# In-place bias rows for the first head, and other moves at the start of an attention and SwiGLU kernel

## The chip, the cores and the metric

The kernel runs on one core of a Trainium2 chip. The metric is the device time of one execution in microseconds (us), as the median over several runs. The profile was taken from one of these executions.

## The reference, cut to what matters

The inputs are q, k, v of shape (8, 8, 576, 64) and s of shape (8, 8, 576): 8 batches of 8 heads, 576 positions, 64 columns per head. The three weight matrices are 512x1536, 512x1536 and 1536x512.

```python
scores = scale * np.matmul(q, k.transpose(0, 1, 3, 2))
s_pos = np.maximum(s, 0.0)
cum = np.cumsum(s_pos, axis=-1)
bias = -(cum[:, :, :, None] - cum[:, :, None, :])
scores = np.where(causal, -1000000000.0, scores + np.minimum(bias, 0.0))
attn = np.exp(scores - np.max(scores, axis=-1, keepdims=True))
attn = attn / (np.sum(attn, axis=-1, keepdims=True) + 1e-09)
x = np.matmul(attn, v)        # heads side by side: 4608 tokens x 512
out = (silu(x @ w_gate) * (x @ w_val)) @ w_out
```

So each score gets a bias that is the difference of two running sums of s, one of the key's position and one of the query's.

## The kernel before

**Tiles.** 64 pairs of batch and head are counted from 0 to 63 (`bh`); head n below means such a pair. Four heads make a half batch (`HB = 4`): heads 0 to 3 are half batch 0, heads 4 to 7 half batch 1, and so on. Queries and keys of a half batch lie transposed in two tiles `KQ[hb % 2][r]`, r = 0 or 1 (lines 91 to 94; in the program kq00 and kq10 for even half batches, kq01 and kq11 for odd ones). Each has 128 partitions, a query part (index 0) and a key part (index 1) of 2 x 576 + 64 columns. The two heads of a row r lie side by side: head e = 0 in columns 0 to 575, head e = 1 in columns 576 to 1151. In tile r the 64 data rows are partitions 64r to 64r + 63. The other 64 are bias rows: four of them hold numbers, the others hold zeros.

**Bias.** The running sums, times 8, are kept in `HL` (64 partitions, one per head) as two bf16 numbers, a high part and the rest, beside rows of 1 and -1. Lines 226 to 232 compute it on VectorE: clamp and scale (226), running sum (227), high part (230), rest (231), and a copy of both for the query side (232). `aug(hb, engs)` (lines 178 to 186) sends to each head four bias rows from `HL` by a DMA (line 183): with the ones and minus ones beside the sums, the score matmul itself adds key sum minus query sum. All four rows of one head are one DMA of 9 KB.

**Scores.** `score_piece(bh, ci)` (lines 338 to 381) computes a head's scores in four pieces, keys on the partitions. `CHUNKS` (lines 56 to 61) lists per piece the blocks of 128 keys and the range of queries. A piece takes a PSUM bank, lays the causal mask into it with a matmul of `lower` (line 353, pieces 0 and 3 of the first 8 heads), adds the scores (line 359), and ScalarE turns it into exps (line 369), which gives the bank back. The fourth piece (`ci = 3`) holds key block 4, and its key operand is always 128 columns wide:

```python
T[:, 1, e * S + 128 * tj : e * S + 128 * (tj + 1)]
```

**Ways into the tiles.** q and k are loaded with positions on partitions and turned by TensorE: for half batch 0 in halves, `row_half(nm, r, eng)` (lines 886 to 890), by transposes into PSUM (line 301) and copies out to `KQ` (lines 314 and 316) on the named engine; for half batch 1 by `half_batch(nm)` (lines 892 to 895, line 287), the r = 0 copies at once, the r = 1 copies by the loop at lines 940 to 942. Half batches 2 to 4 use `prep_one` (line 527), half batch 3 at the places in `PREP_AT` (lines 536 to 539), keyed by half batch and then by the head and piece after which a part stands. Later ones are turned by DMA. `pe_out` copies for both rows share a bank: it is given back after the r = 1 copy. V is loaded in five pieces of 128 positions (`load_v`, line 157) and cast to bf16 with a column of ones beside it (`cast_v`, line 168; `init_vt` sets ones and zeros, lines 189 to 191).

**Order.** The schedule is written out by hand: every engine runs its instructions in the order in which the program lists them, and waits are put in for the data. The first 36 us are lines 188 to 232 and 906 to 980: clear and load, warming matmuls on TensorE (`keep_warm`, line 884), half batch 0, then scores of heads 0 to 7 mixed with half batch 1, values (`values`, lines 901 to 904, matmuls at line 396), transposes of the outputs (`x_pe`, line 446) and the first gate products (`begin`, line 630). From line 1004 on a loop over 9 tiles of 512 tokens runs the feed-forward products (lines 630, 687 and 736) and, between them, the attention of heads 8 to 63 by a running balance (`pump`). `at_item` hooks single steps to items of the first tile: the casts of half batch 3 are hooked to items 7 and 8. PSUM has eight banks; `take()` gives the bank that was given back longest ago.

SyncE issues the DMAs of `nc.sync`: s (line 188), k and q of half batch 0 in halves (line 140), then the bias rows. GpSimd issues k and q of half batch 1 (lines 221 and 222), V of batch 0 (line 915) and the weights (line 332).

## Time and profile before

| What | Value |
|---|---|
| median of 8 runs | 376.38 us (375.62 to 377.71) |
| the profiled execution | 375.62 us, its span 373.9 us |
| TensorE busy | 361.8 us, 97% of the span |
| VectorE, ScalarE, GpSimd busy | 289.1, 240.8, 212.3 us |
| granted clock of TensorE | 0.999 |

| stretch (us) | TensorE busy | VectorE | ScalarE | GpSimd |
|---|---|---|---|---|
| 0 to 12 | 8.17 | 9.95 | 8.61 | 10.86 |
| 12 to 20 | 6.91 | 6.57 | 7.75 | 7.43 |
| 20 to 28.5 | 8.34 | 5.58 | 6.44 | 7.16 |
| 28.5 to 36.7 | 7.38 | 6.68 | 6.48 | 1.94 |
| 36.7 to 60 | 23.14 | 17.93 | 17.65 | 14.15 |
| 60 to 76 | 15.84 | 7.72 | 11.30 | 11.62 |
| 76 to 118 | 41.45 | 32.49 | 34.10 | 21.15 |

Times inside an execution count from the start of its span. A row of the timeline gives start and length in us, then engine, line, operation, tiles and shapes, and in brackets the idle time just before it and what ended it. PE is TensorE, PEld its weight loads, DVE is VectorE, ACT is ScalarE, POOL is GpSimd, SP is SyncE. A row of the waits gives who waited, after the arrow for whom, then us in total, times and the longest. The chain of work that ended last is followed back from the last instruction, at each step to what released it. Releasers are inferred, and the ends of matmuls are modelled.

### The profile page before, as it was taken

To read this page: it belongs to the slowest core of one execution; us is meant where nothing else is said; L and a number is where in the kernel's file an instruction comes from. 1 tells how busy PE (TensorE), PEld (TensorE's weight loads), DVE (VectorE), ACT (ScalarE), POOL (GpSimd) and SP (SyncE) were. 2 spreads that over 40 slices of the span, in tenths; PEclk is the share of its full clock that TensorE was granted. 3 is DMA by queue.
4 is the path that set the end of the run, shared out by engine and by line. 5 is a ranking of instruction groups with operands and counts; after the bars stand their busy time and mean duration, and the time that the engine had idled before them with its cause. 6 is when DMAs were issued, how large, how long until landed. Compare 5 with 4: busy or idle time off the path is not lost.

```text
span 373.9 us, 8757 instructions
## 1 busy us (share of the span) xinstructions
PE 361.8 (97%) x3259; PEld 230.7 (62%) x3300; DVE 289.1 (77%) x578; ACT 240.8 (64%) x471; POOL 212.3 (57%) x325
## 2 busy tenths in 40 slices
PE   7799999999999999999999999999999999999995
PEld 6575556555555556855685558655865585476464
DVE  7967776368984899589967997699858867975984
ACT  8787876788886877588757875686566523323321
POOL 8982565856355647494649464955675516315320
PEclk9999999999999999999999999999999999999999
DMA  7899999999599997896779675994132103002003
GB/s 239 199 262 262 214 266 267 235 338 199 177 178 278 261 264 196 168 283 217 208 166 266 179 177 167 237 224 110 40 119 62 35 20 127 2 0 96 19 0 114
DMA packets 97146, 64.23 MB, mean 172 GB/s; under 512 B 77232, under 2 KB 82736, under 8 KB 97104
## 3 DMA queue, kind: packets, MB, share of 16 engines
q1 hardware_dynamic: 84976, 41.46, 46.7%
q0 software_dynamic: 12128, 22.21, 22.6%
q8 instruction: 26, 0.43, 0.5%
q14 instruction: 16, 0.13, 0.1%
HBM read 37.90 MB, written 19.86 MB: 154 GB/s over the span
## 4 chain that ended last, share of the span: by engine, by line
PE 92%; POOL 2%; DVE 2%; ACT 1%; issue 1%; DMA 1%; DVEq 0%; POOLq 0%
PE bank L630 48%; PE bank L736 17%; PE bank L359 11%; PE bank L396 8%; PE bank L687 5%; ACT pt L369 1%; DMA kq<-HL 1%; PE bank L287 1%; PE bank L446 1%; DVE kq L316 1%; PE bank L353 1%; DVE pp L653 1%; DVE ht L664 0%; POOL kq L214 0%; POOL rawk L140 0%
## 5 line engine op out<-in xcount | busy, mean ns | idle before, releaser
L369 ACT ACTIVATE pt<-bank 128x512 bf16<-128x512 f32 (+1 forms) x256 | 120.4, 509 | 30.2 <-PE bank L359 17.3
L630 PE MATMUL bank<-XT,wg 128*128 128x512 bf16 x418 | 110.5, 379 | 1.2 <-DVE pp L653 0.3
L630 PE MATMUL bank<-XT,wv 128*128 128x512 bf16 x412 | 109.4, 379 | 1.1
L651 ACT ACTIVATE th<-bank 128x512 bf16<-128x512 f32 x108 | 64.7, 599 | 55.5 <-PE bank L630 50.9
L653 DVE SCALAR_TENSOR_TENSOR pp<-th,bank 128x512 bf16<-128x512 bf16 x108 | 73.7, 682 | 18.9 <-ACT th L651 18.4
L664 DVE SCALAR_TENSOR_TENSOR ht<-pp,bank 128x512 bf16<-128x512 bf16 x108 | 74.2, 687 | 10.3
L359 PE MATMUL bank<-kq 128*128 128x128 bf16 (+4 forms) x576 | 75.9, 240 | 1.8 <-DMA kq<-HL 1.3
L673 POOL TENSOR_TENSOR ht<-ht 128x512 bf16<-128x512 bf16 x35 | 40.4, 1154 | 52.3 <-DVE su L671 52.2
L359 PEld LDWEIGHTS <-kq 128*128 128x128 bf16 x576 | 45.8, 98 | 32.0 <-issue 1.9
L630 PEld LDWEIGHTS <-wv 128*128 128x128 bf16 x432 | 38.3, 98 | 36.1 <-issue 0.2
L630 PEld LDWEIGHTS <-wg 128*128 128x128 bf16 x432 | 38.2, 98 | 34.1 <-issue 0.5
L374 POOL TENSOR_SCALAR_AFFINE_SELECT pt<-pt 128x512 bf16<-128x512 bf16 x56 | 36.8, 658 | 29.3 <-ACT pt L369 23.2
L396 PEld LDWEIGHTS <-pt 128*128 128x128 bf16 x960 | 41.6, 98 | 17.4 <-issue 0.3
L396 PE MATMUL bank<-vt,pt 128*128 128x65 bf16 x960 | 46.7, 194 | 0.1
L430 POOL DMA_DIRECT2D xs<-ot x24 | 21.7, 904 | 30.1 <-DVE ot L413 27.8
L736 PEld LDWEIGHTS <-ht 128*128 128x128 bf16 x336 | 31.1, 98 | 4.3
L413 DVE TENSOR_TENSOR ot<-bank,rc 128x320 bf16<-128x320 f32 x64 | 31.5, 492 | 2.2
L183 POOL DMA_DIRECT2D kq<-HL x48 | 28.9, 605 | 0.0
L736 PEld LDWEIGHTS <-su 128*128 128x128 bf16 x252 | 23.5, 98 | 3.3
L687 PE MATMUL bank<-wo,ht 128*128 128x512 bf16 x90 | 24.8, 380 | 0.3
L412 DVE RECIPROCAL rc<-bank 128x5 f32<-128x5 f32 x64 | 12.1, 189 | 15.4 <-PE bank L396 15.0
L801 POOL TENSOR_TENSOR ysb<-ysb 128x512 f32<-128x512 f32 x12 | 15.2, 1270 | 15.3 <-DVE ysb L795 15.3
(93 smaller groups left out, 387.6 us busy)
## 6 DMA issues: line engine op xcount, KB each, us to landing
out_dram<-ysb POOLq DMA_DIRECT2D x32, 256.0 KB, 4.4
rawv<-in_v_dram SPq DMA_DIRECT2D x28, 256.0 KB
rawk<-in_k_dram SPq DMA_DIRECT2D x12, 576.0 KB
rawq<-in_q_dram SPq DMA_DIRECT2D x12, 576.0 KB
xs<-ot POOLq DMA_DIRECT2D x24, 160.0 KB, 3.6
ks<-ck SPq DMA_DIRECT2D x11, 288.0 KB
qs<-cq SPq DMA_DIRECT2D x11, 288.0 KB
rawk<-in_k_dram POOLq DMA_DIRECT2D x3, 576.0 KB, 6.8
```

The source lines that it names most:

```text
L359: nc.tensor.matmul(sc[:, o : o + w], T[:, 1, e * S + 128 * tj : e * S + 128 * (tj + 1)], T[:, 0, e * S + lo : e * S + hi], start=not maske ...
L369: nc.scalar.activation(pt[:, c0 : c0 + n], sc, AF.Exp, scale=0.125)
L374: nc.gpsimd.affine_select(pt[:, 1088:1600], pt[:, 1088:1600], pattern=[[0, 4], [1, 128]], compare_op=ALU.is_ge, fill=zreg, base=0, channel ...
L396: nc.tensor.matmul(av[:, bi * (D + 1) : (bi + 1) * (D + 1)], pt[:, c0 : c0 + 128], VT[b % 2][:, tj, h, :], start=(tj == 0), stop=(tj == bi),)
L413: nc.vector.tensor_mul(ot[:, :, e * D : (e + 1) * D], av3[:, :, 0:D], rc[:, :, None].to_broadcast([128, NCH, D]),)
L630: nc.tensor.matmul(view(bs, TT), w[:, c, f0 : f0 + 128], xt[:, c, :], start=(c == 0), stop=(c == 3),)
L651: nc.scalar.activation(th, pg, AF.Tanh, scale=0.5)
L653: nc.vector.scalar_tensor_tensor(pp, in0=th, scalar=1.0, in1=pg, op0=ALU.add, op1=ALU.mult)
L664: nc.vector.scalar_tensor_tensor(hp[:, 2 * k2 : 2 * k2 + 2, :].rearrange("p a n -> p (a n)"), in0=pp, scalar=0.5, in1=pv, op0=ALU.mult, op ...
L673: (nc.vector if ft == NFT - 1 else nc.gpsimd).tensor_sub(hp[:, 1:3, :], hp[:, 1:4:2, :], hp[:, 0:3:2, :])
L687: nc.tensor.matmul(view(pys[ts_], DM), hps[ft // 2][:, 2 * (ft % 2) + half, c0 : c0 + 128], WO[j][:, ft % WKO, :], start=(ft == 0), stop=( ...
L736: nc.tensor.matmul(ps, lhs(p), rhs(p), start=(first and p == 0), stop=(last and p == NP - 1), skip_group_check=True,)
```

## The change

`HL`, `s_sb` and `c8` get 98 instead of 64 partitions (`LR = 98`). A second load brings s of head 0 to partitions 64 to 97. A column `less` holds -1, and 0 on partitions 64 and 96, so that the instruction that formed the rest now leaves the high part on partitions 64 and 96 and the rest on 65 and 97. GpSimd copies two rows of these, on the partitions where they lie, into kq00, into the key part (64, 65) and the query part (96, 97); ones and minus ones beside them are set by memsets. `aug(0)` leaves head 0 out. After head 3's scores the rows 96 and 97 of the query part are zeroed again, since later heads use four rows from 64 on.

Beside this: pads of half batch 1 and the ones and zeros of V's tile 0 are set by VectorE instead of GpSimd; the first V piece is issued before the in-place copies and the other four right after the cast of the r = 1 queries, ahead of the memset of kq11's bias rows; one of two r = 1 key copies of half batch 0 goes from ScalarE to VectorE; 16 warming matmuls are dropped; the scores of head 0 stand ahead of the r = 1 query transposes; half batch 1 is turned between the scores of heads 1 to 3 in other places; the values of heads 0 and 1 come after the scores of head 6; half batch 3 is prepared half a head later, its casts one item later.

```diff
@@ -78,6 +78,7 @@
     )
 
     NPE = 5
+    LR = 98
     XB = 2
     KS = {i: dram.tile([NR * S, 128], BF16, name=f"ks{i}") for i in range(NPE, NHB)}
     XS = {
@@ -95,15 +96,16 @@
     VT = [const.tile([128, NCH, H, D + 1], BF16, name=f"vt{i}") for i in range(2)]
     ident = const.tile([128, 128], BF16)
     one_s = const.tile([128, 1], FP32)
-    HL = const.tile([BH, 4, 2, S], BF16)
+    HL = const.tile([LR, 4, 2, S], BF16)
     XR = 3 * TT
     XT = const.tile([128, 4, XR], BF16)
     warm = const.tile([128, 1], FP32)
     WS = const.tile([128, NFT // 2, 3, DM // 2], BF16)
     first_sbuf = ExitStack()
     first = first_sbuf.enter_context(tc.tile_pool(name="first", bufs=1))
-    s_sb = first.tile([BH, S], FP32)
-    c8 = first.tile([BH, S], FP32)
+    s_sb = first.tile([LR, S], FP32)
+    c8 = first.tile([LR, S], FP32)
+    less = first.tile([LR, 1], FP32)
     PTP = {0: first, "bufs": 7}
     lower = first.tile([128, 512], BF16)
 
@@ -180,15 +182,19 @@
                 r, e = divmod(hh, 2)
                 r0 = 64 * (1 - r)
                 bh = hb * HB + hh
+                if bh == 0:
+                    continue
                 engs[hh].dma_start(
                     KQ[hb % 2][r][r0 : r0 + 4, :, e * S : (e + 1) * S],
                     HL[bh : bh + 1, :, :, :],
                 )
 
-        nc.sync.dma_start(s_sb, s.rearrange("b h n -> (b h) n"))
-        def init_vt(i):
-            nc.gpsimd.memset(VT[i][:, :, :, D : D + 1], 1.0)
-            nc.gpsimd.memset(VT[i][64:128, 4, :, 0:D], 0.0)
+        nc.sync.dma_start(s_sb[0:BH, :], s.rearrange("b h n -> (b h) n"))
+        nc.sync.dma_start(s_sb[BH:LR, :], s[0, 0:1, :].to_broadcast([LR - BH, S]))
+
+        def init_vt(i, eng=nc.gpsimd):
+            eng.memset(VT[i][:, :, :, D : D + 1], 1.0)
+            eng.memset(VT[i][64:128, 4, :, 0:D], 0.0)
 
         for r in range(NR):
             load_one(0, "k", (r, r + 1))
@@ -197,8 +203,11 @@
         nc.vector.memset(warm, 0.0)
         nc.vector.memset(one_s, 1.0)
         nc.scalar.activation(warm, warm, AF.Exp)
-        nc.vector.memset(HL[:, 0:2, 0, :].bitcast(FP32), ONES2)
-        nc.vector.memset(HL[:, 2:4, 1, :].bitcast(FP32), NEGS2)
+        nc.vector.memset(HL[0:BH, 0:2, 0, :].bitcast(FP32), ONES2)
+        nc.vector.memset(HL[0:BH, 2:4, 1, :].bitcast(FP32), NEGS2)
+        nc.vector.memset(less, -1.0)
+        for p in (64, 96):
+            nc.vector.memset(less[p : p + 1, :], 0.0)
         make_identity(nc, ident)
         nc.gpsimd.memset(lower, 0.0)
         nc.gpsimd.affine_select(
@@ -206,9 +215,9 @@
             compare_op=ALU.is_ge, fill=nc.gpsimd.to_reg(MASKED), base=0, channel_multiplier=-1,
         )
 
-        def pads(i):
+        def pads(i, eng=nc.gpsimd):
             for r in range(2):
-                nc.gpsimd.memset(KQ[i][r][64 * r : 64 * r + 64, :, NR * S :], 0.0)
+                eng.memset(KQ[i][r][64 * r : 64 * r + 64, :, NR * S :], 0.0)
 
         for r in range(2):
             nc.gpsimd.memset(aug_rows(0, r)[:, 1, :], 0.0)
@@ -216,20 +225,29 @@
                 KQ[0][r][64 * (1 - r) : 64 * (1 - r) + 64, 0, :],
                 one_s[0:64, 0:1].to_broadcast([64, NR * S + 64]), 0.0,
             )
+            if r == 0:
+                nc.gpsimd.memset(KQ[0][0][96:98, 1, 0:S].bitcast(FP32), NEGS2)
         pads(0)
+        nc.gpsimd.memset(KQ[0][0][64:66, 0, 0:S].bitcast(FP32), ONES2)
         nc.vector.memset(aug_rows(1, 0), 0.0)
         for nm in ("k", "q"):
             load_one(1, nm, eng=nc.gpsimd)
-        init_vt(0)
-        pads(1)
+        pads(1, nc.vector)
+        init_vt(0, nc.vector)
+        load_v(0, (0,), nc.gpsimd)
 
         nc.vector.tensor_scalar(s_sb, s_sb, 0.0, 8.0, ALU.max, ALU.mult)
         nc.vector.tensor_tensor_scan(
-            c8, one_s[0:BH, 0:1].to_broadcast([BH, S]), s_sb, 0.0, ALU.mult, ALU.add
+            c8, one_s[0:LR, 0:1].to_broadcast([LR, S]), s_sb, 0.0, ALU.mult, ALU.add
         )
         nc.vector.tensor_copy(HL[:, 0, 1, :], c8)
-        nc.vector.tensor_sub(HL[:, 1, 1, :], c8, HL[:, 0, 1, :])
-        nc.vector.tensor_copy(HL[:, 2:4, 0, :], HL[:, 0:2, 1, :])
+        nc.vector.scalar_tensor_tensor(
+            HL[:, 1, 1, :], in0=HL[:, 0, 1, :], scalar=less, in1=c8,
+            op0=ALU.mult, op1=ALU.add,
+        )
+        for p, kq in ((64, 1), (96, 0)):
+            nc.gpsimd.tensor_copy(KQ[0][0][p : p + 2, kq, 0:S], HL[p : p + 2, 1, 1, :])
+        nc.vector.tensor_copy(HL[0:BH, 2:4, 0, :], HL[0:BH, 0:2, 1, :])
 
         SP4 = [nc.sync] * 4
         GP4 = [nc.gpsimd] * 4
@@ -534,7 +552,7 @@
             seconds.append(lambda: pe_out(hb, nm, g, 1, eng))
 
         PREP_AT = {
-            2: {(1, 0): 0, (1, 2): 2, (2, 0): 1, (2, 2): 3},
+            2: {(1, 2): 0, (2, 0): 2, (2, 2): 1, (3, 0): 3},
             3: {(1, 3): 0, (2, 1): 1, (2, 3): 2, (3, 1): 3},
         }
 
@@ -883,11 +901,11 @@
             for _ in range(n):
                 nc.tensor.matmul(view(spare, 128), ident, ident, start=True, stop=True)
 
-        def row_half(nm, r, eng):
+        def row_half(nm, r, eng, eng1=None):
             for g in range(2):
                 pe_transpose_half(0, nm, g, r)
             for g in range(2):
-                pe_out(0, nm, g, r, eng)
+                pe_out(0, nm, g, r, (eng, eng1 or eng)[g])
 
         def half_batch(nm):
             for g in range(2):
@@ -911,14 +929,14 @@
         row_half("q", 0, nc.vector)
         cast_half(0, "k", 1, nc.scalar)
         cast_half(0, "q", 1, nc.gpsimd)
+        load_v(0, range(1, 5), nc.gpsimd)
         nc.gpsimd.memset(aug_rows(1, 1), 0.0)
-        load_v(0, range(5), nc.gpsimd)
         w_load("g", 0)
         aug(1, SP4)
-        keep_warm(10)
-        row_half("k", 1, nc.scalar)
+        keep_warm(4)
+        row_half("k", 1, nc.scalar, nc.vector)
+        scores(0)
         row_half("q", 1, nc.vector)
-        keep_warm(10)
         cast_one(1, "k", nc.vector)
         cast_one(1, "q", nc.vector)
         for c in range(3):
@@ -931,16 +949,19 @@
         for nm in ("g", "v"):
             w_load(nm, 1, 0)
         load_one(3, "k", eng=nc.gpsimd)
-        scores(0)
+        scores(1)
+        for ci in (0, 1):
+            score_piece(2, ci)
         half_batch("k")
-        scores(1)
+        for ci in (2, 3):
+            score_piece(2, ci)
         half_batch("q")
-        scores(2)
         scores(3)
         for nm in ("k", "q"):
             for g in range(2):
                 pe_out(1, nm, g, 1, nc.vector)
         cast_v(0, 4, nc.vector)
+        nc.gpsimd.memset(KQ[0][0][96:98, 0, 0:S].bitcast(FP32), 0.0)
         aug(2, SP4)
         cast_one(2, "k", nc.gpsimd)
         cast_one(2, "q", nc.gpsimd)
@@ -950,8 +971,8 @@
         init_vt(1)
         scores(4)
         scores(5)
+        scores(6)
         values(0, 1)
-        scores(6)
         values(2, 3)
         scores(7)
         aug(3, SP4)
@@ -997,8 +1018,8 @@
             hook[n].append(lambda: f(*args))
 
         at_item(2, prep_one, 2, 2)
-        at_item(7, cast_one, 3, "k", nc.gpsimd)
-        at_item(8, cast_one, 3, "q", nc.gpsimd)
+        at_item(8, cast_one, 3, "k", nc.gpsimd)
+        at_item(9, cast_one, 3, "q", nc.gpsimd)
         at_item(10, w_load, "o", 0)
         at_item(12, w_load, "o", 1)
         for tt in range(NTT):
```

## Prediction

> **What bounds the kernel now.** I read the page first (TensorE 97% busy, 12 us idle in all), then the busy time by stretch, to see where that idle time lies: 3.83 us in 0 to 12, 1.09 in 12 to 20, 0.16 in 20 to 28.5, 0.82 in 28.5 to 36.7, under 1.5% from 36.7 to 300. The waits show no wait of TensorE of 0.15 us or more after 36. So the change can matter only where it stands, in the first 36 us; from there a shift of TensorE's work is a shift of the end. The chain that ended last, there:
>
> ```profile
> 7.51 3.71 DMA kq<-HL
> 11.26 0.83 PE bank L359 x8
> ...
> 12.67 1.71 ACT pt L369 x4
> ...
> 15.06 1.09 ACT pt L369 x2
> ...
> 18.35 0.71 PE bank L359 x8
> ...
> 20.05 0.92 PE bank L396 x30
> ```
>
> A row is start, length, what. Head 0's scores wait for bias rows that a DMA brings (issued 7.51, landed 11.22). Then ScalarE's exps set the pace to about 18; from 18.35 TensorE runs without a gap. The start is set by VectorE, by the waits of SyncE's queue and of the whole start:
>
> ```profile
> SPq L183 <- DVE HL L232: 4.0, 1, 4.0
> PE bank L359 <- DMA kq<-HL: 1.3, 1, 1.3
> ACT pt L369 <- PE bank L359: 1.9, 1, 1.9
> ```
>
> VectorE computes HL (lines 226 to 232, ending at 7.41); only then are bias rows sent. What VectorE does afterwards, in its timeline:
>
> ```profile
> 3.71 0.47 DVE L226 TENSOR_SCALAR s_sb<-s_sb 64x576 f32<-64x576 f32 x1
> 6.87 0.54 DVE L232 COPY HL<-HL 64x1152 bf16<-64x1152 bf16 x1
> 7.33 1.43 DVE L316 COPY kq<-bank 64x640 bf16<-64x640 bf16 x2
> 9.07 1.46 DVE L316 COPY kq<-bank 64x640 bf16<-64x640 bf16 x2 [0.31 <-PE bank L301]
> 10.56 0.76 DVE L246 CAST ck<-rawk 128x1152 bf16<-128x1152 f32 x1
> 11.43 0.93 DVE L246 CAST cq<-rawq 128x1152 bf16<-128x1152 f32 x1
> 12.55 5.75 DVE L316 COPY kq<-bank 64x640 bf16<-64x640 bf16 x8 [0.19 <-PE bank L287]
> ```
>
> This is nearly unbroken to 18.30. The pair at 9.07 are the row-1 queries of half batch 0, the last eight the copies of half batch 1. Heads 4 and 5 need them twice: as data (first four) and for the PSUM banks that the last four free. They end only about 1.2 us before TensorE takes the last such bank (third piece of head 5, about 19.5). VectorE is the near-bound here, and the change gives it more.
>
> **What the Trainium skill says.** "DMA: Bandwidth & Descriptors", section "Queues, rings and completion order": a DMA engine alternates between queues by packet, but the semaphore increment lands only after every earlier write of that engine, whatever its queue. The trace agrees in part: packets of SyncE's queue appear from 9.4 on, yet head 0's rows count as landed at 11.22, after the software queue's K and Q of half batch 1 thin out at 10.6. "VectorE: DVE Perf Modes", section "Zero memsets can be issued as uint32 (trn2)": a memset takes one cycle per element whatever the type; here 576 elements took 538 ns and 1216 took 1072, 0.9 ns each. "TensorE: Matmul & The Clock Gate", Part 1: an idle window of about 3.4 us halves TensorE's clock; the granted clock was 1.00 in every stretch here, so no run shows it.
>
> **The change, part by part.**
>
> 1. *VectorE ahead of HL.* Added: three memsets of `less` (0.06 each, as line 197), pads of half batch 1 (2 x 64 elements, 0.12 each), vt ones (40 elements, 0.10), vt zeros (512 elements, 0.48 by the rate above): 1.0 us. The 0.29 us idle ahead of line 220 can take part of it; I count 0.85 (0.6 to 1.0). The chain itself (3.70 us, 3.71 to 7.41) keeps its lengths, since they go with elements, not partitions; the scalar_tensor_tensor is priced as the 0.75 of line 231 (0.5 to 0.9). HL ends at 8.26.
> 2. *Head 0's rows in place.* GpSimd's two copies of 2x576 follow the scalar_tensor_tensor (about 7.7); as the 128x576 cast of line 256 (0.66, at least the 0.52 of a 512-element memset) they end at 9.0. VectorE's two copies of row-0 queries now run 8.3 to 9.7 and are later. So head 0's scores start at 9.75 instead of 11.26: 1.5 us earlier.
> 3. *But only three of its four pieces.* The fourth takes keys 512 to 639 of the tile that holds heads 0 and 1 side by side, 576 columns each: 64 of those columns are head 1's, whose rows still come by DMA. Its weight load waits for that DMA in the new order too, and TensorE issues in order. Before, head 1's rows were issued at 8.38 and the fourth piece ran at 11.94, so at most 3.56 us. Now they are issued first, at 8.26 + 0.10; 8.36 + 3.56 = 11.9. Bounds: packets appear 2 us after the issue, so 10.7 at the earliest; the s of 34 more partitions (78 KB) and the early V piece (256 KB) add 0.33 MB ahead, at the 415 GB/s of 9.0 to 9.5 0.8 us, so 12.7.
> 4. *What stands behind that wait.* The transposes of row-1 queries, run at 8.57 before, now stand behind the fourth piece: start 12.0. VectorE copies them 0.5 after (as 8.57 to 9.07): 12.5 instead of 9.07. From there to the last copy of half batch 1 before took 18.30 - 9.07 = 9.2; less the 0.1 of gaps it is 9.1: 21.6. The copy of row-1 keys that moves from ScalarE (0.72) fits into VectorE's wait between 9.7 and 12.5. TensorE reaches the third piece of head 5 at 21.6, and its end at 21.9, where before it was 20.05.
> 5. *After that* the order has the same work: scores 6 and 7, values, transposes, 6.6 us without a gap before (20.1 to 26.7: 6.60 busy). Values 0 and 1 move behind scores 6, which asks no bank later than head 5's first exp. So the 1.9 us stay. Had VectorE not been late, ScalarE's earlier start would be the gain.
> 6. *Queues.* SyncE: one load of s more (0.56, like line 140's first), one bias DMA less (0.82); K and Q of half batch 0 start 0.5 later, half hidden by ScalarE's zero fills, which end at 4.79. GpSimd: two memsets more (0.3 each), pads and vt off it (1.5), V piece 0 early (0.98), two copies (1.3); its cast of row-1 queries ends at about 9.7 instead of 8.5, well before 12.0. The memset of tile kq11 now follows the V issues, to 14.8 instead of 9.56; the bias rows of heads 6 and 7 queue behind it on SyncE, land at about 19, and are asked at 22. Weight loads leave at 19.4 as before. All at nothing; uncovered, the SyncE shift would cost up to 0.5.
> 7. *Sixteen warming matmuls fewer:* hidden by the waits, 0.
> 8. *Half batch 3 later:* the same transposes and copies between other items. TensorE has no wait there, and head 12 comes at least three pieces after the last: 0. If its copies came late, 0.7 each.
> 9. *The zeroing of head 0's rows* (2x288 on GpSimd, 0.3) waits for head 3's scores; behind it the casts of half batch 2, used 4 us later: 0.
>
> Sum: +1.9 us (item 4), all else 0. Against the profiled execution (375.62, span 373.9) that is 377.5; that one was the fastest of eight, so for the median I add it to 376.38: 378.3.
>
> **Rivals.** *Bias rows land early.* With the bulk loads out of the way head 1's rows could be there at 10.7 or before. For: a 9 KB transfer needs little. Then item 4 gives 0.7 (landing minus 10.0), and down to 10.4, where the first three pieces end, +0.4: 376.8 to 377.1, no change that the measurement tells. *ScalarE's exps set the end (faster).* For: they run almost unbroken from 11.70 to 25.2 and carry the chain to 18. If their start decides, it moves from 11.70 to about 10.2: -1.5, 374.9; if they pause for head 1's rows, -0.9, 375.5. It decides if VectorE's last copy ends by about 18.4, so that no bank is waited for. Against: even with no wait VectorE has 1.0 + 0.72 us more to do by then, and at most 0.8 of gaps to fill with it: 19.2. I would have to be wrong in two durations. *The change doesn't do what it says* holds of the fourth piece (item 3) and is in the forecast.
>
> **How the numbers follow.** About 0.2%, 0.75 us, is what a measurement of this kernel tells from no change. Forecast (slower, own range 377.2 to 379.3 from landings of 10.8 to 12.7 with 0.2 on top): 0.64. Early landing: 0.19. Exps: 0.17. The range reaches down to 375.4, so that most of the last case and the top of the first are left out.
>
> **What would show it.** Right: TensorE idle for 1.3 to 2 us inside head 0's scores, waiting for DMA kq<-HL at about 11.9; VectorE's pair of row-1 query copies at 12.5; the last copy of half batch 1 ending at 21 to 22; the values of heads 6 and 7 ending near 28.6 instead of 26.7. Wrong: rows landed before 10.5, a VectorE chain that ends before 19, or new TensorE idle time later than 36 us. Worse than the range would be a granted clock below 1.00 while TensorE waits.

## The result, and the profile after

The changed kernel takes 380.7 us (median of 11 runs, 379.47 to 381.39), the kernel before on the same chips 376.57 us (32 runs). The ratio is 1.0097 with a 95% interval of 1.0076 to 1.0118: slower by about 3.65 us (4.1 between the two medians). The direction was forecast (slower, 378.3); the size is about twice the forecast and above the range's top of 379.3. The profiled execution took 380.37 us, its span is 378.5 us; before it was 375.62 and 373.9, the fastest of its eight, so the two traces lie 4.6 us apart.

In the changed kernel line numbers have moved: the score matmuls are line 377 (359 before), the exps 387 (369), the copies from PSUM 334 on VectorE and 332 on ScalarE (316, 314), the half-batch casts 264 (246), the part casts 272 (254), the copy that ends `HL` 250 (232), the bias transfers 187 (183).

VectorE's timeline, kernel after (start, length, engine, line, what; in brackets the idle time before, and what ended it):

```profile
5.90 0.46 DVE L239 TENSOR_SCALAR s_sb<-s_sb 98x576 f32<-98x576 f32 x1 [0.86 <-DMA s_sb<-in_s_dram]
9.14 0.45 DVE L250 COPY HL<-HL 64x1152 bf16<-64x1152 bf16 x1
...
13.68 1.46 DVE L334 COPY kq<-bank 64x640 bf16<-64x640 bf16 x2 [1.76 <-PE bank L319]
15.17 1.41 DVE L264 CAST ck<-rawk 128x1152 bf16<-128x1152 f32 x1
16.50 1.62 DVE L264 CAST cq<-rawq 128x1152 bf16<-128x1152 f32 x1
18.15 5.63 DVE L334 COPY kq<-bank 64x640 bf16<-64x640 bf16 x8
```

The chain starts with s at 5.90, not 3.71; the pair of row-1 query copies runs at 13.68, not 9.07; the two casts take 3.0 us, not 1.7; the last copy of half batch 1 ends at 23.78, not 18.30. TensorE's timeline shows where the late start comes from:

```profile
7.21 1.17 PE L319 MATMUL bank<-ident,ck 128*64 128x128 bf16 x9 [2.17 <-ACT ck L272]
...
11.42 1.46 PE L377 MATMUL bank<-kq 128*128 128x128 bf16 x8
...
13.04 0.20 PE L377 MATMUL bank<-kq 128*128 128x64 bf16 x1
13.17 0.69 PE L319 MATMUL bank<-ident,cq 128*64 128x128 bf16 x9
...
22.48 0.38 PE L371 MATMUL bank<-lower,ident 128*128 128x512 bf16 x1 [0.41 <-DVE kq L334]
...
23.84 0.38 PE L377 MATMUL bank<-kq 128*128 128x320 bf16 x2 [0.26 <-DVE kq L334]
...
57.43 0.19 PE L414 MATMUL bank<-vt,pt 128*128 128x65 bf16 x1 [0.28 <-POOL vt L170]
```

TensorE idles 2.17 us for the first keys (0.55 before, nine transposes at 5.41), head 0's scores start at 11.42 (before 11.26), and the row-1 query transposes stand behind head 0's fourth piece at 13.17. In head 5 TensorE waits twice for the copies of half batch 1, the second time until 23.84; from there its timeline shows no wait until 31.5, as in the kernel before from 18.35 to 27.5. The chain that ended last has the same steps: the transfer of head 1's bias rows, the fourth piece and the transposes behind it, VectorE's pair and cast, and its last copies, for which head 5 waits:

```profile
9.69 3.30 DMA kq<-HL
13.04 0.20 PE bank L377
13.24 0.41 PE bank L319 x5
13.68 1.46 DVE kq L334 x2
15.17 1.42 DVE ck L264
...
19.53 1.41 DVE kq L334 x2
...
20.96 2.83 DVE kq L334 x4
...
23.84 0.38 PE bank L377 x2
```

**One ruler for all runs** is ScalarE's timeline. It makes 32 exps for heads 0 to 7, 13.52 us of work. In the kernel before they run in one piece; ScalarE's timeline, kernel before:

```profile
11.70 13.52 ACT L369 ACTIVATE pt<-bank 128x512 bf16<-128x512 f32 x32 [1.88 <-PE bank L359]
```

The same in the kernel after:

```profile
12.09 1.69 ACT L387 ACTIVATE pt<-bank 128x512 bf16<-128x512 f32 x4 [0.65 <-PE bank L377]
14.44 2.67 ACT L387 ACTIVATE pt<-bank 128x512 bf16<-128x512 f32 x6 [0.66 <-PE bank L377]
17.57 0.71 ACT L387 ACTIVATE pt<-bank 128x512 bf16<-128x512 f32 x2 [0.45 <-PE bank L377]
19.33 1.69 ACT L387 ACTIVATE pt<-bank 128x512 bf16<-128x512 f32 x4 [1.05 <-PE bank L377]
21.41 5.14 ACT L387 ACTIVATE pt<-bank 128x512 bf16<-128x512 f32 x12 [0.38 <-PE bank L377]
27.57 1.69 ACT L387 ACTIVATE pt<-bank 128x512 bf16<-128x512 f32 x4 [1.02 <-PE bank L377]
```

They start only 0.39 us later, but pause five times for scores, and end at 27.57 + 1.69 = 29.26 in place of 25.22: 4.04 us, of which 3.65 are pauses (29.26 - 12.09 - 13.52). What follows the last exp takes 378.5 - 29.26 = 349.2 us, before 373.9 - 25.22 = 348.7. So 4.0 of the 4.6 us between the traces arise before the last exp and 0.5 after it. The pauses tell how late the scores come; they are not themselves the cause. The last one, 1.02 us, falls where TensorE does the values of heads 0 to 3 ahead of head 7's scores, and TensorE waits for nothing there. The table gives both parts for every run: start of the first exp, pauses (end less start less 13.52), end of the last, and the rest of the span, all from one profiled execution each; the time is the median of all its runs.

| run | time, us | ratio to before, 95% | first exp | pauses | end | rest |
|---|---|---|---|---|---|---|
| before | 376.57 | | 11.70 | 0 | 25.22 | 348.7 |
| after | 380.70 | 1.0097 (1.0076 to 1.0118) | 12.09 | 3.65 | 29.26 | 349.2 |
| e1_spread64 | 380.70 | 1.0111 (1.0085 to 1.0138) | 11.41 | 4.02 | 28.95 | 349.2 |
| e2_rows_distinct | 380.61 | 1.0118 (1.0090 to 1.0146) | 12.12 | 3.65 | 29.29 | 349.2 |
| e3_load_only | 377.72 | 1.0031 (1.0017 to 1.0045) | 12.98 | 0.59 | 27.09 | 348.4 |
| e4_prep_back | 379.78 | 1.0078 (1.0052 to 1.0105) | 11.94 | 3.84 | 29.30 | 348.5 |
| e5_old_order | 379.94 | 1.0092 (1.0068 to 1.0115) | 12.58 | 1.82 | 27.92 | 349.2 |
| e6_four_rows | 380.41 | 1.0100 (1.0076 to 1.0124) | 11.34 | 4.23 | 29.09 | 349.7 |
| e7_warm | 380.85 | 1.0117 (1.0100 to 1.0134) | 11.39 | 4.78 | 29.69 | 349.2 |
| e8_rows_and_order | 380.88 | 1.0126 (1.0091 to 1.0162) | 13.67 | 1.99 | 29.18 | 349.7 |
| e9_vector_early | 380.78 | 1.0113 (1.0061 to 1.0166) | 10.62 | 6.73 | 30.87 | 349.6 |
| e10_casts_first | 379.64 | 1.0091 (1.0063 to 1.0119) | 10.51 | 7.16 | 31.19 | 350.5 |
| e11_all | 377.78 | 1.0028 (1.0003 to 1.0052) | 10.44 | 5.96 | 29.92 | 348.6 |
| e12_prep_late | 376.21 | 0.9993 (0.9976 to 1.0010) | 11.38 | 0 | 24.90 | 350.0 |
| e13_order_prep | 378.98 | 1.0055 (1.0034 to 1.0076) | 13.63 | 1.16 | 28.31 | 348.5 |
| e14_and_v_back | 379.48 | 1.0063 (1.0030 to 1.0097) | 13.48 | 1.80 | 28.80 | 348.8 |
| e15_and_zero_back | 379.85 | 1.0081 (1.0057 to 1.0105) | 13.52 | 1.56 | 28.60 | 349.9 |
| e16_all_v_back | 380.41 | 1.0086 (1.0057 to 1.0114) | 10.38 | 2.75 | 26.65 | 353.2 |
| e17_v_between | 378.81 | 1.0074 (1.0054 to 1.0094) | 10.71 | 2.91 | 27.14 | 349.4 |
| e18_v_back_prep_late | 379.39 | 1.0078 (1.0064 to 1.0092) | 10.63 | 2.52 | 26.67 | 351.0 |

Each run's ratio is to runs of the kernel before on its own chip (medians there 376.4 to 377.1). The profiled executions of e9, e10, e11 and e16 lie 1.1 to 4.2 us above the medians of their runs, those of the kernel before and of e5 about 1.0 us below, so a difference of 1 us between two traces need not be one between two kernels.

### The profile page after: what moved, and what is told of

It is laid out like the page before. It is cut to its first block, busy times and chain, and to the rows that moved or that the text cites. A ratio compares the mean times of both kernels' runs of the same rounds, so it can differ in the third digit from the quotient of the medians.

```text
span 378.5 us, 8745 instructions
## 1 busy us (share of the span) xinstructions
PE 364.2 (96%) x3244; PEld 231.8 (61%) x3284; DVE 292.8 (77%) x586; ACT 240.3 (63%) x470; POOL 213.1 (56%) x326
## 4 chain that ended last, share of the span: by engine, by line
PE 88%; DVE 4%; POOL 3%; issue 2%; ACT 1%; DMA 1%; DVEq 0%; POOLq 0%; ACTq 0%
PE bank L648 46%; PE bank L754 17%; PE bank L377 10%; PE bank L414 8%; PE bank L705 5%; DVE kq L334 2%; PE bank L305 1%; DMA kq<-HL 1%; PE bank L464 1%; ACT pt L387 1%; DVE pp L671 1%; POOL vt L170 1%; DVE ht L682 1%; DVE ck L264 0%; ACT kq L332 0%
## 5 line engine op out<-in xcount | busy, mean ns | idle before, releaser
L377 PE MATMUL bank<-kq 128*128 128x128 bf16 (+4 forms) x576 | 76.8, 242 | 1.2 <-DVE kq L334 0.6
L431 DVE TENSOR_TENSOR ot<-bank,rc 128x320 bf16<-128x320 f32 x64 | 31.5, 492 | 2.2
L397 POOL TENSOR_SCALAR_AFFINE_SELECT pt<-pt 128x64 bf16<-128x64 bf16 x56 | 14.8, 264 | 17.7 <-ACT pt L387 17.6
```

What stands on the lines that cost most here:

```text
L377: nc.tensor.matmul(sc[:, o : o + w], T[:, 1, e * S + 128 * tj : e * S + 128 * (tj + 1)], T[:, 0, e * S + lo : e * S + hi], start=not maske ...
L431: nc.vector.tensor_mul(ot[:, :, e * D : (e + 1) * D], av3[:, :, 0:D], rc[:, :, None].to_broadcast([128, NCH, D]),)
```

## The experiments

My first theory was that the load of s to 34 more partitions delays all that SyncE loads behind it, and that this lateness is most of the loss. The rivals were the new order near head 0's scores, the later preparation of half batch 3, and TensorE's slow start.

### The load

e3 puts the load alone into the kernel before, its result unused:

```diff
-    s_sb = first.tile([BH, S], FP32)
+    s_sb = first.tile([LR, S], FP32)
...
+        nc.sync.dma_start(s_sb[BH:LR, :], s[0, 0:1, :].to_broadcast([LR - BH, S]))
```

> The kernel before, with only the second load of s (head 0's row to 34 more partitions, used by nothing) put behind the first. Load theory: k lands near 6.4 instead of by 4.70, ScalarE and TensorE start half batch 0 about 1.7 us later; the bias rows of head 0, which set the start before (11.22), are moved less, since VectorE waits only for the first load; so 0.7 to 1.7 us slower, 377.3 to 378.3. Wait theory: the load is hidden, no change, 376.6.

Measured: 377.72 us, 1.2 us slower by the ratio. ScalarE's timeline of this run:

```profile
6.68 0.67 ACT L256 CAST ck<-rawk 128x576 bf16<-128x576 f32 x1 [1.90 <-DMA rawk<-in_k_dram]
...
12.98 1.69 ACT L371 ACTIVATE pt<-bank 128x512 bf16<-128x512 f32 x4 [0.47 <-PE bank L361]
15.15 11.94 ACT L371 ACTIVATE pt<-bank 128x512 bf16<-128x512 f32 x28 [0.48 <-PE bank L361]
```

A load that nobody reads brings the keys at 6.68, not 4.70. So the load alone costs 1.2 us in the kernel before, as forecast, which is a third of the loss.

e1 makes the 34 partitions 64; e2 reads 34 different rows in place of one row 34 times:

```diff
-    LR = 98
+    LR = 128                                     # e1
...
-        nc.sync.dma_start(s_sb[BH:LR, :], s[0, 0:1, :].to_broadcast([LR - BH, S]))
+        nc.sync.dma_start(s_sb[BH:LR, :], s.rearrange("b h n -> (b h) n")[0 : LR - BH, :])   # e2
```

> The changed kernel, but s of head 0 goes to 64 more partitions instead of 34 (98 becomes 128). Load theory: a load to 34 partitions is carried by few DMA engines and holds up what is queued behind it; 64 partitions spread over all of them. Then k of the first half lands near 4.9 us instead of 6.48, VectorE's first use of s starts near 5.1 instead of 5.90, and the time falls by 1.3 to 2 us, to about 379. Rival (the same 2.3 KB row of DRAM read many times is what is slow): 64 reads of it are worse than 34, k lands after 6.5 and the time stays at 380.7 or rises. Rival (the wait of head 0's fourth piece and the added VectorE work alone): no change, 380.7.

> The changed kernel, but the second load of s takes 34 different rows (heads 0 to 33) instead of head 0's row 34 times; head 0's bias is then made from other heads' s on three of its four rows. Load theory with few engines: still 34 partitions, so no change: k lands near 6.5, time 380.7. Rival (one row read many times): k lands near 4.9 and the time falls by 1.3 to 2 us, to about 379. Wait theory: no change.

Measured: with 64 partitions the keys land at 5.73 (34: 6.48), though nearly twice the bytes are asked; with 34 different rows at 6.51. So it is the number of partitions that makes the load slow, not the one row. The Trainium skill, "DMA: Bandwidth & Descriptors", section "Why a DMA increments its semaphore by 16 and not by 1", says that a DMA is spread over the largest number of engines up to 16 that divides its outermost dimension, which makes 2 for 34 partitions and 16 for 64. The landings agree, but no trace here shows the engines one by one, and the rate doesn't decide: from 4 to 5 us the changed kernel moves 53 GB/s at a DMA share of 0.24 and the one with 64 partitions 297 at 0.93, but the one with 34 different rows, whose keys are just as late, 359 at 1.05. And the time stays at 380.7 us, where the theory had about 379. The last exp ends only 0.3 us earlier: what is gained at the keys is lost in longer pauses. VectorE still starts on s at 5.28 there (3.71 in the kernel before). The load theory can't be the main one.

### The stage's other suspects, one at a time

e7 fills TensorE's wait for keys with 36 more warming matmuls; e6 loads s of head 0 only to partitions 64, 65, 96 and 97, in two small transfers behind the first keys and queries, with zeros on the 30 others.

```diff
-        keep_warm(32)
+        keep_warm(68)                            # e7
...
-        nc.sync.dma_start(s_sb[BH:LR, :], s[0, 0:1, :].to_broadcast([LR - BH, S]))
+        nc.vector.memset(s_sb[BH:LR, :], 0.0)
...
+            if r == 0:
+                for p in (64, 96):
+                    nc.sync.dma_start(
+                        s_sb[p : p + 2, :], s[0, 0:1, :].to_broadcast([2, S])
+                    )                            # e6
```

> The changed kernel with 68 in place of 32 warming matmuls at the start, which fills TensorE's 2.2 us wait for the keys. If TensorE's half rate from 7 to 13 us after that wait costs time: nine transposes take 0.69 us again, head 0's scores end some 1 us earlier, VectorE's second pair of query copies starts near 12.7 in place of 13.7, time 379.9 us (379.5 to 380.4). Rival (the rate is not on the path, or it stays low for another reason): same as the changed kernel, 380.4 to 381.

> The changed kernel, with s of head 0 loaded to the four partitions that are used (64, 65, 96, 97) in two small transfers after the first keys and queries, and zeros on the 30 between. Theory of the load: keys land at 4.7 to 5.2 us as in the kernel before, s at 5.0 to 5.5, TensorE's first wait falls from 2.2 to under 1 us, its matmuls from 7 us on run at their full rate (nine transposes in 0.69 us, not 1.17), and 1.2 to 2 us come back: 378.9 us (378.4 to 379.5). Rival (the order after it holds the time, as the load spread over 64 partitions suggests): 380.2 to 380.9.

Measured: neither helps (380.85 and 380.41); neither of the gains came. In e7 the transposes have their full rate again, and the pair of copies stays where it was. Its TensorE, then its VectorE:

```profile
7.46 0.69 PE L319 MATMUL bank<-ident,ck 128*64 128x128 bf16 x9
...
13.07 0.20 PE L377 MATMUL bank<-kq 128*128 128x64 bf16 x1 [1.26 <-DMA kq<-HL]
```

```profile
13.71 1.47 DVE L334 COPY kq<-bank 64x640 bf16<-64x640 bf16 x2 [2.13 <-PE bank L319]
```

0.69 in place of 1.17 us, and 13.71 as against 13.68: TensorE's half rate is off the path. A faster TensorE only waits longer, 1.26 us, for head 1's bias rows. In e6 the transposes start at 5.40 as before the change, but head 0's scores start at 10.92, after a wait of 1.88 us for VectorE's query copies, and the fourth piece waits for its transfer until 12.51. s of head 0 comes behind the keys there, and `HL` is ready at 9.42 (9.59 in the changed kernel). So keys on time change nothing as long as VectorE and the transfer of head 1's rows hold the same place.

e5 puts the old order back in this stretch, e4 the old times of half batch 3:

```diff
         row_half("k", 1, nc.scalar, nc.vector)
-        scores(0)
         row_half("q", 1, nc.vector)
...
-        scores(1)
-        for ci in (0, 1):
-            score_piece(2, ci)
+        scores(0)
         half_batch("k")
-        for ci in (2, 3):
-            score_piece(2, ci)
+        scores(1)
         half_batch("q")
+        scores(2)                                # e5
...
-            2: {(1, 2): 0, (2, 0): 2, (2, 2): 1, (3, 0): 3},
+            2: {(1, 0): 0, (1, 2): 2, (2, 0): 1, (2, 2): 3},    # e4; casts at items 7 and 8
```

> The changed kernel with the hand-written order of the kernel before in one stretch: the query transposes and copies of the heads of half batch 0 with r = 1 stand ahead of head 0's scores again, and half batch 1's transposes stand between the scores of heads 0, 1 and 2. The in-place rows, the load to 34 more partitions and the later half batch 3 stay. Theory (half batch 1's copies are late because the second pair of query copies queues behind head 0's scores): that pair starts near 12 us in place of 13.7, the last of the eight copies ends near 21.5 in place of 23.8, time 378.6 us (378.0 to 379.4). Rival (the late loads and the slow matmuls set the copies, whatever the order): last copy 23 or later, time 380.3 or more.

> The changed kernel with half batch 3 prepared and cast where the kernel before does it. In the trace of the change TensorE lost about 0.5 us more between 46 and 58 us than before in 42 to 54, and the chain runs there through ScalarE's and VectorE's copies and GpSimd's V casts. If the later preparation causes this: 0.4 to 0.7 us faster than the change, about 380.1. If it follows from the later start or the order on GpSimd: no change, 380.7.

Measured: e5 379.94 (0.8 us less than after between the medians), e4 379.78 (0.9 less). The interval of each overlaps that of the changed kernel, so neither gain alone is clear of noise. In the traces e5 acts ahead of the last exp (27.92 in place of 29.26), e4 behind it (a rest of 348.5 in place of 349.2). ScalarE in e5:

```profile
12.58 1.69 ACT L387 ACTIVATE pt<-bank 128x512 bf16<-128x512 f32 x4 [1.43 <-PE bank L377]
15.63 10.18 ACT L387 ACTIVATE pt<-bank 128x512 bf16<-128x512 f32 x24 [1.36 <-PE bank L377]
26.23 1.69 ACT L387 ACTIVATE pt<-bank 128x512 bf16<-128x512 f32 x4 [0.42 <-PE bank L377]
```

The first exp is 0.5 us later than in the changed kernel, and yet the last ends 1.3 earlier, since 24 exps run without a pause. An early first head is worth nothing when the heads behind it come late.

VectorE did in e5 what the theory said (the pair at 11.81, the last copy ending at 20.91), and yet the time missed the forecast 378.6. The traces give a reason: these copies then no longer hold TensorE. With the changed order (after, e1, e2, e4, e6, e7, e9, e10) TensorE waits for them in head 5; with the old order (e5, e8, e11, e13 to e18) it has no such wait, and 20 or 24 exps run in one piece, at ScalarE's pace, but that piece starts late (between 15.6 and 19.4 us).

e13 takes both edits, e12 puts the later half batch 3 alone into the kernel before:

```diff
-            2: {(1, 0): 0, (1, 2): 2, (2, 0): 1, (2, 2): 3},
+            2: {(1, 2): 0, (2, 0): 2, (2, 2): 1, (3, 0): 3},    # e12; casts at items 8 and 9
```

> The changed kernel with the order near head 0's scores and the times of half batch 3 both as in the kernel before. If the two causes add up (0.8 and 0.9 us): 379.0 us (378.5 to 379.5). If both stand for the same late stage: 379.7 or more.

> The kernel before with only half batch 3 prepared later (its transposes half a head later, its two casts one item later). If this costs what undoing it in the changed kernel gave back (0.9 us): 377.4 us (377.0 to 377.8). If it costs only where the stages before are late: 376.3 to 376.8.

Measured: e13 378.98, 1.7 us less than after between the medians (1.6 by the ratios, whose intervals just touch): what the two single gains add up to. e12 376.21, no change. So the later half batch 3 costs nothing that the median shows in the kernel before, and some 0.9 us in the changed one. The profile of e12 does show waits that the kernel before has not; TensorE's timeline:

```profile
40.15 0.45 PE L287 MATMUL bank<-ident,ck 128*128 128x128 bf16 x5 [0.63 <-POOL ck L246]
...
53.88 0.19 PE L396 MATMUL bank<-vt,pt 128*128 128x65 bf16 x1 [0.28 <-POOL vt L168]
```

GpSimd's cast of the keys comes later (38.95, after 0.98 us of waiting for the keys to land; 37.05 in the kernel before), and so do the casts of V behind it in its queue. The second wait is the one at 57.43 in the changed kernel; e4 and e13 have none of the two. Why the medians of e12 don't show it stays open.

### Doing it better, and what comes in the way

e8 is e5 and e6 together. e9 loads the four partitions ahead of the keys and gives the zeroing that the change put on VectorE back to GpSimd. e10 also moves half batch 1's casts into VectorE's wait. e11 also has the row-1 query transposes ahead of head 0's fourth piece, half batch 1's transposes in the old place and half batch 3 at the old times.

```diff
+        nc.vector.memset(s_sb[BH:LR, :], 0.0)
+        for p in (64, 96):
+            nc.sync.dma_start(s_sb[p : p + 2, :], s[0, 0:1, :].to_broadcast([2, S]))   # e9
-        pads(1, nc.vector)
-        init_vt(0, nc.vector)
         load_v(0, (0,), nc.gpsimd)
+        pads(1)                                  # e9; init_vt(0) later on GpSimd
...
+        cast_one(1, "k", nc.vector)
+        cast_one(1, "q", nc.vector)
         row_half("q", 1, nc.vector)              # e10
-        cast_one(1, "k", nc.vector)
-        cast_one(1, "q", nc.vector)
...
-        scores(0)
+        for ci in range(3):
+            score_piece(0, ci)
         row_half("q", 1, nc.vector)
+        score_piece(0, 3)                        # e11
```

> The two edits together: s of head 0 to four partitions only, and the order of the kernel before around head 0's scores. If late loads and late order are both causes and add up: last copy of half batch 1 near 19 to 20 us, time 377.3 us (376.7 to 378), of which 0.9 is the later half batch 3. If either alone is all that matters, this is no faster than the better one of the two.

> The changed kernel with VectorE's start relieved: s of head 0 goes to its four partitions in two small transfers right behind the load of s (zeros on the 30 partitions between), and the zeroing that the change gave to VectorE goes back to GpSimd. Theory (VectorE's chain, late by 2.2 us, holds head 0's scores and all behind them): the bias rows are ready near 8.5 us in place of 9.6, head 0's scores start near 10.3 in place of 11.4, the last copy of half batch 1 ends near 22.8 in place of 23.8, time 379.6 us (379.0 to 380.1). Rival (the order behind head 0's scores takes the gain back): 380.2 to 381.

> The kernel of the vector-early run, and half batch 1's two casts ahead of the second pair of query copies on VectorE, where it waits near 2 us for that pair's transposes. Theory (those copies wait behind head 0's scores, and VectorE's wait is what makes half batch 1 late): the casts fill the wait, the last copy of half batch 1 ends near 21 in place of 22.8, time 378.4 us (377.8 to 379.2). Rival (the casts on VectorE wait for their keys, or slow beside GpSimd, or the exps then set the pace): less than 0.5 us faster than the vector-early run.

> The kernel of the casts-first run; TensorE does the second query transposes ahead of head 0's fourth piece, which waits for a transfer, and half batch 1's transposes stand where the kernel before had them; half batch 3 is prepared at its former times. If the four causes add up: last copy of half batch 1 near 19 us, time 376.5 us (375.8 to 377.3), no slower than the kernel before. Rival (a cause is missing): 377.5 or more.

Measured: 380.88, 380.78, 379.64 and 377.78, where the theories had 377.3, 379.6, 378.4 and 376.5: all four missed. TensorE's timeline of e8 shows what stands in its way:

```profile
12.10 0.69 PE L324 MATMUL bank<-ident,cq 128*64 128x128 bf16 x9 [3.18 <-POOL cq L279]
```

The row-1 query transposes, ahead of head 0's scores again, wait for a cast that GpSimd does behind the two in-place copies, and these wait for `HL` (ready at 10.07). The same wait is 0.72 us in e5 and 0.69 in e13. In the profiled execution of e9 `HL` is ready at 8.52 and the first exp runs at 10.62, the start that the change was to give, and all is lost again at one place. TensorE's timeline of e9:

```profile
10.05 0.97 PE L378 MATMUL bank<-kq 128*128 128x128 bf16 x8
...
14.64 0.23 PE L378 MATMUL bank<-kq 128*128 128x64 bf16 x1 [3.59 <-DMA kq<-HL]
```

Head 1's bias rows were issued at 8.62 and land near 14.6: 6.0 us for 9 KB, where the changed kernel needs 3.30. The prediction had taken 3.56 as if the time from issue to landing were the transfer's own. The profiled e11 has the same wait, 3.5 us at 15.13; that execution is 2.7 us above e11's median, and how much of the wait the others have, no trace here shows.

e14 puts V's five pieces back in their old place in e13, e15 also VectorE's zeroing; e16 does to e11 what e14 does to e13:

```diff
-        load_v(0, (0,), nc.gpsimd)
-        load_v(0, range(1, 5), nc.gpsimd)
         nc.gpsimd.memset(aug_rows(1, 1), 0.0)
+        load_v(0, range(5), nc.gpsimd)           # e14, e16
...
-        pads(1, nc.vector)
-        init_vt(0, nc.vector)
+        init_vt(0)
+        pads(1)                                  # e15
```

> As the run before it, and all five pieces of V issued where the kernel before issues them. Theory (the sooner piece of V shares the DMA engines with half batch 1's queries and head 1's bias rows): queries and bias rows land some 0.5 to 1 us earlier, time 378.5 us (378.0 to 378.9). Rival (V's place is not on the path): same as the run before it within 0.3 us, or slower because V's casts come later.

> As the run before it, and the zeroing that the change gave to VectorE back on GpSimd: what stays of the change is the load to 34 more partitions, head 0's rows in place, one key copy on VectorE in place of ScalarE, fewer warming matmuls and the place of head 6's scores. Since s lands only near 5.9 us, VectorE's earlier end of zeroing should give nothing: same as the run before it within 0.3 us. If the rest costs no more than the load alone does: 377.7 to 378.1 us. If head 0's rows in place cost something of their own: above 378.3.

> The run of all edits (377.8 us), with all five pieces of V issued where the kernel before issues them. Theory of the DMA engines' share: half batch 1's keys and queries land near 11.6 and 12.7 us in place of 12.7 and 14.2, head 1's bias rows near 13.5 in place of 15.1, TensorE's wait of 3.5 us falls to some 2, time 376.8 us (376.3 to 377.3). Rival (the transfers are late for another reason): 377.6 or more.

Measured: 379.48, 379.85 and 380.41. e14 and e16 missed what their theories had. e15 is above its 378.3: what it keeps of the change costs 1.9 us more than the load alone (ratios of 1.0081 and 1.0031, with intervals apart). So head 0's rows in place, the one key copy, the fewer warming matmuls and the place of head 6's scores cost something among them; which of them was not separated. e16 shows the stage without that wait, and its price. Its TensorE, then its GpSimd:

```profile
11.43 0.20 PE L377 MATMUL bank<-kq 128*128 128x64 bf16 x1
...
42.47 0.45 PE L305 MATMUL bank<-ident,ck 128*128 128x128 bf16 x5 [2.51 <-POOL ck L264]
```

```profile
41.28 1.13 POOL L264 CAST ck<-rawk 128x1152 bf16<-128x1152 f32 x1 [4.33 <-DMA rawk<-in_k_dram]
```

With V out of the way the fourth piece runs at 11.43 without a wait, half batch 1's keys are there by 10.63 (12.72 in e11), and the last exp ends at 26.65, 2.6 us before that of the changed kernel. But half batch 3's keys then land late, and TensorE waits 2.51 us at 42; its granted clock falls to 0.87 from 36.7 to 46 us. The rest grows to 353.2. It is not GpSimd's time that is short here: it stands idle for 4.33 us until the keys are there. Their load, in its queue behind V and the weights, was issued at 25.29, 1.5 us later than in e11, and took 15.9 us to land. What holds it is not shown; SyncE's loads of the next batch's V begin at 26.32 there and at 29.59 in e11. In e15 TensorE's wait is 1.37 us, and GpSimd's for the keys 3.20.

e18 prepares half batch 3 later in e16, by the lines that e4 took out; e17 takes e11, issues V's five pieces in between and gives the key copy back to ScalarE:

```diff
-        load_v(0, (0,), nc.gpsimd)
...
-        load_v(0, range(1, 5), nc.gpsimd)
+        load_v(0, range(5), nc.gpsimd)
...
-        row_half("k", 1, nc.scalar, nc.vector)
+        row_half("k", 1, nc.scalar)              # e17
```

> The run of all edits with V's pieces issued late, and half batch 3 prepared at the changed kernel's later times. If the 2.5 us wait for GpSimd's cast came from GpSimd being late, it shrinks to under 1 us and the time falls by 1.5 to 2.5 us, to 378.2 us (377.6 to 379). If the wait moves with the preparation: 379.8 or more.

> The run of all edits with all five pieces of V issued by GpSimd right after its query cast (ahead of its zeroing, behind the loads of half batch 1 and the copies of head 0's rows), and the second key copy of the heads with r = 1 back on ScalarE. If V's place is the conflict (sooner delays half batch 1's loads, later delays half batch 3's cast): head 1's bias rows land near 11.5 us, no wait for GpSimd's cast near 42 us above 0.5, last copy of half batch 1 near 20, time 376.9 us (376.3 to 377.5). If something else holds it: 377.6 or more.

Measured: e18 379.39, with the wait at 42 down to 1.28. Against e16 that is no clear gain (ratios of 1.0078 and 1.0086, with intervals that overlap), and the keys land no sooner: the cast runs at 41.37, after GpSimd waited 1.63 us for them. The later preparation only asks for them later. e17 378.81, with TensorE's wait at 0.50 and the fourth piece at 11.53, as its theory said, but at 378.81 the time is above 377.6, from where on its text put it down to something else. In e17 VectorE waits twice for half batch 1 (0.42 and 0.61 us), and its query cast takes 2.21 us. No version of the changed kernel beats the kernel before. The nearest is e11, still 0.03 to 0.52% slower.

## Where the prediction failed, and where it held

The path was right and its terms were too small. The forecast had head 5's third piece at 21.6 us and the trace has it at 23.84. `HL`'s rows were issued 1.33 us later than forecast (9.69 for 8.36), head 1's transfer took 0.26 less (3.30 for 3.56), and VectorE's casts took 1.3 more. Behind the last exp half batch 3, set at nothing, adds more.

**The reading of the bound held.** VectorE's near-unbroken chain to the last copy of half batch 1 was named as what sets the end, and it does: the last copy ended at 23.78, head 5's scores at 24.3, and the values of heads 6 and 7 near 30.7, where the kernel before had 18.30, 20.05 and 26.7.

**Item 1, VectorE ahead of HL, failed in size.** Foreseen were +0.85 us and an end of `HL` at 8.26. It ended at 9.59, 2.2 us later than before. The zeroing is busy for what was worked out (1.1 us), but it ended at 5.03, 1.46 us later than VectorE's memset of line 220 before, and s came only at 5.90: the wait of 0.86 us comes on top. The chain from there kept its length, as forecast (3.69 us on 98 partitions, 3.70 on 64).

**Item 6, "All at nothing; uncovered, the SyncE shift would cost up to 0.5", is the step that failed first.** The load was priced by its issue (0.56 us) and its bytes. The keys behind it come 1.8 us later (6.48 for 4.70), and VectorE waits for s itself. Alone it costs 1.2 us (e3).

**Items 2 and 3.** GpSimd's two copies took 0.67 and 0.95, not 0.66 each, and ended at 10.83, not 9.0; head 0's scores started at 11.42, not 9.75. The fourth piece did stand behind head 1's transfer, which landed at 12.99 (forecast 11.9, bounds 10.7 to 12.7). The wait itself, foreseen as 1.3 to 2 us, was 0.3, because everything else was late too. It is 1.26 us in e7, and 3.6 and 3.5 in the profiled e9 and e11.

**Item 4, mechanism right, two terms too small.** The pair started at 13.68 in place of 12.5 (+1.2). From there to the last copy took 10.1 us in place of 9.1 (+1.0), which the two casts more than explain: 3.0 us for 1.7. Together 2.2: 23.8 in place of 21.6.

**Item 5, "So the 1.9 us stay", holds in kind.** The shift at the values of heads 6 and 7 is 4.0 us, the same as that of the last exp. The rival "ScalarE's exps set the end" did not come: it needed VectorE's last copy by about 18.4. Nor would an earlier first exp have been the gain: in e6 and e7 it is 0.7 us earlier than in the changed kernel, and the last one ends at 29.1 and 29.7 (29.26 there).

**Item 8, half batch 3 later at 0, failed.** In the changed kernel it is some 0.9 us (e4, between the medians), behind the last exp. It was costed on TensorE, and its casts on GpSimd, ahead of V's casts, were not followed: the one wait of that kind in the trace is 0.28 us at 57.43, and where the rest arises stays open.

**Item 7** (sixteen warming matmuls fewer at 0) was not tested by itself; 36 more at the start gained nothing (e7).

**The sum.** Beside the 3.65 us stand 1.2 for the load (measured in the kernel before), 1.7 for order and half batch 3 together, and so some 0.8 for the rest of the change. That last share is a remainder; e15 has 1.9 us for it, with half batch 3's keys landing late besides. No run takes the in-place rows or the place of head 6's scores back by itself. And the parts don't simply add: undoing the load alone in the changed kernel (e1, e6) gave nothing.

**What the V piece and VectorE's zeroing are for.** In e13 to e15, where order and times are the old ones, taking each back made it slower, by 0.5 and 0.4 us in the medians, differences that the intervals don't separate. That these moves relieve GpSimd, which has the in-place copies besides, is a reading that no run shows.

## What to carry to other kernels

Take one engine's stream of a stage as a ruler and measure it from first to last item: an earlier first item is worth nothing if the later items are starved. When a fix takes one wait away and the time stays, look for the next wait at the same place: here the copies on VectorE, the transfer of head 1's rows, a cast on GpSimd and the exps took turns. Price a small load at the head of a queue by when the loads behind it land, not by its bytes. And when issues of transfers move, follow each transfer to its consumer: a stall of 2.5 us appeared 30 us behind the edit.

## What the runs showed of the hardware

**A load to 34 partitions held up the loads behind it.** With it, one row 34 times or 34 different rows, the keys landed 1.8 us later (6.48 and 6.51 for 4.70). The same load to 64 partitions cost 1.0 us (5.73), two loads of two partitions ahead of the keys 0.4 (5.10, e9), behind the first keys and queries nothing (4.69, e6).

**A 9 KB transfer took 2.9 to 6.5 us from issue to use**, with the loads that were in flight beside it: at most 2.9 in e16 and 3.0 in e17 (V issued later), 3.0 in e6, 3.3 in the changed kernel, 3.5 in e7, 6.0 in e9 and 6.5 in e11. The place of V's first piece alone doesn't make the difference: e6, e7 and the changed kernel issue it at 6.5 us, e9 and e11 at 6.8. The profiled e9 and e11 took more time than their medians, and in which queue or engine the transfer stands is not shown.

**TensorE's half rate, and how the granted clock shows it.** After a wait of 2.17 us nine transposes took 1.17 us and eight score matmuls 1.46 (0.69 and 0.83 in the kernel before), and the granted clock reads 1.00. But time without a record of the clock is counted as 1.00. The changed kernel's first record is the rise to 1.00 at 12.72 us (at 4.53 in the kernel before), and nine transposes at 13.17 take 0.69 again. Where there are records, they agree with the durations: in e13 the clock is 1.00 from 4.93, 0.50 from 8.34 and 1.00 from 15.17; nine transposes take 0.69 at 7.08 and 1.17 at 9.60. The Trainium skill, "TensorE: Matmul & The Clock Gate", Part 1, tells of a halved clock after an idle window of about 3.4 us. In e13 the changes lie 3.41 us or twice that apart, but TensorE need not be idle all that time: it was busy for 1.33 of the 3.41 us before the fall at 8.34, and in e16 for 1.07 before one at 43.54. In the kernel before it was busy for 2.06 us from 7.94 to 11.35, and the clock stayed.

**A cast of 128x1152 from fp32 took from 0.76 to 2.21 us on VectorE**, by the run and its place in it. In the changed kernel GpSimd's timeline has this beside the two slow casts:

```profile
14.82 1.14 POOL L933 MEMSET kq<- 64x1216 f32 x1
15.88 1.00 POOL L350 DMA_DIRECT2D wg<-in_moe_w_gate_dram  x1
16.88 2.27 POOL L170 CAST vt<-rawv 128x512 bf16<-128x512 f32 x3
```

GpSimd's three casts take 0.76 each there, one alone 0.62. Whether the two engines slow each other is not shown: in e17 the cast of 2.21 us ran while GpSimd only issued transfers. What slows it was not settled.
